# An RWKV-and-FFN kernel on one core: another order for its ramp, and GpSimd's constants in another order

## The chip, the cores and the metric

The kernel runs on one core of one Trainium2 chip. Its time is the device time of one execution in microseconds (us). Before the change the median of 3 runs is 554.37 us (554.30 to 554.86). The engines are named as the profile names them: PE (TensorE matmul; PEld is its weight load), DVE (VectorE), ACT (ScalarE), POOL (GpSimd), SP (SyncE). SP, POOL and ACT also issue transfers; "SPq" marks such an issue.

## The reference, cut to what matters

```python
for t in range(768):                       # B=4, H=8, D=48
    cur = einsum('bhd,bhe->bhde', u * kt, vt)
    y[:, :, t] = einsum('bhd,bhde->bhe', rt, state + cur)
    state = wt[..., None] * state + einsum('bhd,bhe->bhde', kt, vt)
x = y.transpose(0, 2, 1, 3).reshape(3072, 384)
h = x @ w_in                               # 384 x 2048
out = (h * sigmoid(1.702 * h)) @ w_out     # 2048 x 384
```

A linear recurrence with a decay per channel, and then a feed-forward layer over all 3072 tokens, all in float32.

## The kernel before, in words

The sequence is cut into 24 chunks of 128 tokens, 6 per batch entry. `chunk(t)` (L208) is a generator of 12 steps; the order calls one step with each token `a`t. Steps 1 and 2 scan the decays on DVE (L221 and L227, with the constants `d1r` and `d1f`) and form r·k (`rku`, L234); step 3 makes the scaled k and r (`kq`, L242 and L243); step 4 is PE's `ps_d` (L249: r·k times `hm`, the masks with u); step 5 copies that to `s` (L252) and decays the state (L259); step 6 transposes k (`ps_t`, L265) and ACT copies it to `kt` (L267); step 7 is ACT's `am`, eight diagonals (L274); step 8 is `ps_u`, k·v (L281 and L282), and the new state (L287); step 9 is `ps_s`, k·q (L293); step 10 puts `ps_s` into `am` above the diagonal (DVE, L296, twice); step 11 is `ps_y` (L306, and L313 where there is a state); step 12 splits `ps_y` into two float32r parts in `x` (ACT L191, DVE L192). `measure` (token `m`, L197) is bookkeeping of ranges on ACT.

The FFN is cut into tasks, each one slice f of 128 hidden units for 2, 3 or 4 chunks of tokens. `g`j is the first product of task j (PE, L343 to L345, nine matmuls), `h`j the GELU in two parts (ACT L354 and L355, DVE L356), `y`j the second product (PE, L369 to L371, nine matmuls). Two PSUM buffers hold first products, so `g`j+2 waits for both ACT reads of `h`j. The first tasks are 256 tokens wide. Before a group's tasks may run, small transfers fill 16-row strips of `x` from other rows of it (`fill_x`, L331, tokens `x1` for chunks 0 and 1, `x3` for chunks 2 and 3).

The weights come as packed 64-bit numbers in twelve pieces (even ones w_in, odd ones w_out). Token `f`i issues piece i's transfer into one of three staging buffers `st` (L161 or L163); tokens `w`i convert it in four steps: ACT L177 and L178, DVE L180 and L183, ACT L185 (`wih` or `woh`), DVE L187 (`wil` or `wol`). `l`t issues a chunk's loads (`wkr_t` on SP and POOL, or on SP and ACT for chunk 0; `v_t` on SP), `M` the two small transfers of the masks into `hm` (L424, L425), `u` that of `u_sb`.

All of this is laid out by hand: the string `RAMP` is a list of tokens, executed in that order until task 42, and `rest()` goes on by rule from there, leaving out what the string has done. Every engine executes its own instructions in the order in which the tokens emit them, so the string fixes the order on each engine and each issuing queue. The constants ahead of the string (`ident`, `after`, `hm`, `d1r`, `d1f`, `acc`) are written by POOL and are not part of it.

Of the kernel before, what the change touches and what calls it, by code (L numbers as in the profile page):

```python
# [8 lines left out]
F32 = mybir.dt.float32  # L9
F32R = mybir.dt.float32r  # L10
BF16 = mybir.dt.bfloat16
# [11 lines left out]
NP = H // 2  # L23
R = 2 * D
HB = 64
R2 = HB + D
C = P
CB = S // C
NT = NTOK // C
CW = C + 1  # L30
# [30 lines left out]

FIRST = 42
RAMP = """
l0 l0 M a0 l1 a0 a0 a0 a0 m0 a0 a1 a1 a1 l0 f0 m0 a0 a0 a0 a0 a1 a1 w0 m1 l2 w0 a2 a0 l1 a0 a1 a1 f1 a1 w0 a1
a2 l3 a2 w1 m1 f2 m2 m2 a2 a2 w0 a1 f3 w1 a3 a2 a1 a1 w2 a2 a3 w2 w1 l2 l3 x1 a2 w2 w1 a2 a3 a3 a3 g1 g0 a2 w2
m3 w3 a2 l4 h0 a4 a2 a3 w3 a3 a3 a4 g2 m3 w3 l4 a3 f4 a3 w3 h1 h2 w4 w4 a4 y0 a3 f5 f6 w5 g3 a3 w4 g4 y1 f7 w4
h3 w5 a4 a4 y2 h4 w6 g5 h5 a4 w5 y3 y4 x3 g7 w5 g6 w6 w7 h6 h7 w7 f8 y5 g8 w6 y7 a4 h8 y6 w6 a4 w7 g9 f9 g10
h9 w8 a4 y8 g11 w7 w8 h10 h11 y9 g12 w9 l5 g13 y10 y11 w8 w9 h12 f10 g14 f11 h13 y12 w8 h14 w9 y13 g16 w10 y14
w9 g15 h16 g18 a4 h15 m4 g17 w11 w10 h17 a5 m4 a4 y15 h18 a5 l6 l6 y16 y17 w10 g19 h19 l5 g20 a5 w11 a5 h20
w10 g21 u m5 a5 a5 a6 y18 y19 m5 w11 w11 h21 y20 g22 y21 a4 a6 a5 l7 a6 a5 a5 m6 a5 h22 a6 g23 h23 y22 a6 a5  # L70
a5 a7 a6 a6 l7 g24 a7 a6 a6 g25 x5 h24 a7 a7 m6 y23 a6 g26 l8 m7 a6 a7 a8 l8 a7 h25 h26 y24 a6 a7 a8 a8 g27
y25 g28 a7 a7 h28 h27 m7 y26 g30 a7 g29 y27 m8 h29 l9 g31 h30 y28 l9 y29 a8 a7 g32 l10 a8 h31 m8 a9 g33 a9 a8
y30 a9 h32 h33 y31 g34 a8 l10 y32 y33 m9 h34 g35 y34 h35 a7 g36 h36 g37 a8 a8 h37 g38 y35 a8 g39 a9 y36 a8 a9
y37 h38 a8 l11 m9 y38 h39 g40 x8 a9 g41 l11 h40 h41 y39
"""
WIDE = 512
assert sum(CHUNKS) == NT
# [3 lines left out]
def rwkv_ffn_kernel(ctx: ExitStack, tc, wkr, vp, vrk, ub, w_in, w_out, masks, vt, uc, out):  # L81
    nc = tc.nc
    V, A, G, T = nc.vector, nc.scalar, nc.gpsimd, nc.tensor

    cp = ctx.enter_context(tc.tile_pool(name="cp", bufs=1))
# [6 lines left out]
    at = fast.enter_context(tc.tile_pool(name="at", bufs=1))  # L92


    ident = cp.tile([P, P], F32, name="ident")
    make_identity(nc, ident)
    after = cp.tile([P, C], F32, name="after")
# [7 lines left out]
    G.memset(hm, 0.0)  # L105
    u_heads = hm[:, 2:].rearrange("r (p h) -> r p h", h=2)
    u_sb = cp.tile([P, DM], F32, name="u_sb")
    d1r = cp.tile([R2, NP, CW], BF16, name="d1r")
    G.memset(d1r, 0.0)
    G.memset(d1r[:, :, C : C + 1], 1.0)  # L110
    d1f = cp.tile([R2, NP, CW], F32, name="d1f")
    G.memset(d1f, 0.0)

    def by_head(dst, src, other=None):

# [465 lines left out]
```

## Time and profile before

| | |
|---|---|
| median of 3 runs | 554.37 us |
| the profiled execution | 553.65 us, its span 552.1 us |
| PE busy | 527.5 us (96%), 4038 matmuls |
| DVE, ACT busy | 288.6 us (52%), 291.0 us (53%) |
| PE first busy | 8.35 us |
| last wait of PE | ends at 66.19 us |
| last matmul of the FFN | starts at 545.54 us |
| transfers | 48.17 MB, DMA engines full in most of the first 65 us |

The span runs from the first to the last instruction of the execution. A mean share hides the stages here: in the first 66 us PE waits in many places while DVE and ACT work nearly without a pause from about 40 us on; after that PE is never idle until the last 7 us.

### The profile page before, as it was taken

The numbers are of one execution on the slowest core, as the hardware profiler recorded it, in microseconds if no ns is written. First come the engines' busy times: TensorE is split into PE (matmuls) and PEld (weight loads), VectorE is DVE, ScalarE is ACT, GpSimd is POOL, SyncE is SP. The second block draws the span as 40 slices with busy tenths as digits, with TensorE's granted clock in tenths as the row PEclk, the third lists the DMA queues.
The fourth block names the chain that finished last, engine by engine and source line by source line (L and its number), as shares of the span: only waits on it lengthen the run. The fifth ranks groups of instructions, "written<-read, shape, count | busy, mean of one in ns | idle before, by whom it ended". The sixth has DMA issues, their size and how long they took to land.

```text
span 552.1 us, 10054 instructions
## 1 busy us (share of the span) xinstructions
PE 527.5 (96%) x4038; PEld 493.7 (89%) x4038; DVE 288.6 (52%) x470; ACT 291.0 (53%) x686; POOL 34.6 (6%) x75
## 2 busy tenths in 40 slices
PE   1978999999999999999999999999999999999995
PEld 1857999988999999999999999999999999999995
DVE  4889977956643445536445445436445345321210
ACT  3778988656654364455454453455453563423222
POOL 3120210001001000000001000010001000010000
PEclk9999999999999999999999999999999999999998
DMA  8979797305632133143143241242242300011001
GB/s 176 248 186 214 174 230 183 67 1 130 180 94 59 37 93 60 36 115 99 39 93 81 78 94 34 61 114 72 67 94 55 104 1 1 2 23 43 1 0 49
DMA packets 18854, 48.17 MB, mean 87 GB/s; under 512 B 3312, under 2 KB 10064, under 8 KB 18800
## 3 DMA queue, kind: packets, MB, share of 16 engines
q1 hardware_dynamic: 15376, 36.02, 25.6%
q0 software_dynamic: 3296, 11.13, 10.0%
q8 instruction: 34, 0.56, 0.5%
q10 hardware_dynamic: 128, 0.30, 0.2%
q14 instruction: 20, 0.16, 0.1%
HBM read 40.36 MB, written 4.72 MB: 82 GB/s over the span
## 4 chain that ended last, share of the span: by engine, by line
PE 89%; DVE 4%; DMA 3%; issue 1%; ACT 1%; POOL 1%; SPq 0%; DVEq 0%; POOLq 0%
PE po L369 14%; PE ph L343 12%; PE ph L345 12%; PE ph L344 12%; PE po L371 12%; PE po L370 12%; PE ps_y L306 4%; PE ps_s L293 4%; PE ps_y L313 4%; DMA st<-in_w_out 3%; PE ps_u L281 1%; PE ps_t L265 1%; DVE st L180 1%; PE ps_d L249 1%; DVE c L183 1%
## 5 line engine op out<-in xcount | busy, mean ns | idle before, releaser
L356 DVE TENSOR_TENSOR gl<-gf,gh 128x384 fp32r<-128x384 f32 (+2 forms) x138 | 72.5, 529 | 209.0 <-ACT gf L355 208.5
L354 ACT ACTIVATE gh<-ph 128x384 fp32r<-128x384 f32 (+2 forms) x138 | 64.7, 469 | 195.6 <-PE ph L345 190.6
L369 PE MATMUL po<-gh,woh 128*128 128x384 f32 (+2 forms) x414 | 140.4, 339 | 0.0
L343 PE MATMUL ph<-x,wih 128*128 128x384 f32 (+2 forms) x414 | 135.5, 327 | 0.0
L345 PE MATMUL ph<-x,wil 128*128 128x384 f32 (+2 forms) x414 | 134.5, 325 | 0.0
L344 PE MATMUL ph<-x,wih 128*128 128x384 f32 (+2 forms) x414 | 134.4, 325 | 0.0
L371 PE MATMUL po<-gl,woh 128*128 128x384 f32 (+2 forms) x414 | 133.9, 324 | 0.3 <-DVE gl L356 0.3
L370 PE MATMUL po<-gh,wol 128*128 128x384 f32 (+2 forms) x414 | 134.1, 324 | 0.0
L369 PEld LDWEIGHTS po<-gh,woh 128*128 128x128 f32 x414 | 78.0, 188 | 6.6 <-issue 2.8
L343 PEld LDWEIGHTS ph<-x,wih 128*128 128x128 f32 x414 | 78.8, 190 | 1.7 <-issue 0.6
L345 PEld LDWEIGHTS ph<-x,wil 128*128 128x128 f32 x414 | 78.7, 190 | 0.8
L344 PEld LDWEIGHTS ph<-x,wih 128*128 128x128 f32 x414 | 78.7, 190 | 0.7
L371 PEld LDWEIGHTS po<-gl,woh 128*128 128x128 f32 x414 | 78.0, 188 | 1.3 <-DVE gl L356 0.5
L370 PEld LDWEIGHTS po<-gh,wol 128*128 128x128 f32 x414 | 78.2, 189 | 0.6
L355 ACT ACTIVATE gf<-ph 128x384 f32<-128x384 f32 (+2 forms) x138 | 64.0, 464 | 0.0
L274 ACT ACTIVATE am<-ident,s 128x128 f32<-128x128 f32 x192 | 58.9, 401 | 0.0
L221 DVE TENSOR_TENSOR_SCAN lp<-wkr_t,d1r 112x516 f32<-112x516 f32 x24 | 29.4, 1224 | 8.1 <-POOL d1r L110 4.8
L296 DVE COPY_PREDICATED am<-after,ps_s 128x512 f32<-128x512 int32 x48 | 32.4, 729 | 1.6 <-PE ps_s L293 1.6
L293 PE MATMUL ps_s<-kq 48*128 48x128 f32 x384 | 31.4, 304 | 0.1
L306 PE MATMUL ps_y<-am,v_t 128*64 128x128 f32 (+1 forms) x384 | 29.3, 291 | 2.3 <-DVE am L296 1.2
L293 PEld LDWEIGHTS ps_s<-kq 48*128 48x128 f32 x384 | 26.2, 204 | 5.2 <-issue 4.1
L306 PEld LDWEIGHTS ps_y<-am,v_t 128*64 128x64 f32 (+1 forms) x384 | 22.3, 136 | 8.2 <-DVE rk_t L237 2.2
(62 smaller groups left out, 483.3 us busy)
## 6 DMA issues: line engine op xcount, KB each, us to landing
wkr_t<-in_wkr SPq DMA_DIRECT2D x23, 385.2 KB, 5.8
wkr_t<-in_wkr POOLq DMA_DIRECT2D x23, 288.9 KB, 5.8
st<-in_w_out SPq DMA_DIRECT2D x6, 1024.0 KB, 11.8
rk_t<-in_vrk SPq DMA_DIRECT2D x16, 384.0 KB, 4.6
v_t<-in_vrk SPq DMA_DIRECT2D x24, 192.0 KB, 6.1
out_t<-ob SPq DMA_DIRECT2D x18, 192.0 KB, 1.9
st<-in_w_in POOLq DMA_DIRECT2D x6, 384.0 KB, 7.8
st<-in_w_in SPq DMA_DIRECT2D x6, 384.0 KB, 10.8
```

The costliest lines, as they stand in the source:

```text
L274: A.activation(x_[:, p], ident, AF.Copy, scale=s[:, 2 * p + h : 2 * p + h + 1])
L293: T.matmul(ps[h][:, p], kf[head(h), p], qf[head(h), p], start=True, stop=True)
L306: T.matmul(ps[at_ : at_ + m, p], v_[:, c : c + m], am[h][:, p], start=p == 0, stop=sf is None and p == NP - 1, skip_group_check=True,)
L343: T.matmul(ph, h_, xs[i][:, 0, c, cs], start=c == 0, stop=False)
L344: T.matmul(ph, h_, xs[i][:, 1, c, cs], start=False, stop=False)
L345: T.matmul(ph, l_, xs[i][:, 0, c, cs], start=False, stop=c == NM - 1)
L354: A.activation(gh, ph, AF.Gelu_apprx_sigmoid, scale=1.0 / W_SCALE)
L355: A.activation(gf, ph, AF.Gelu_apprx_sigmoid, scale=1.0 / W_SCALE)
L356: V.tensor_tensor(gl, gf, gh.bitcast(F32), op=ALU.subtract)
L369: T.matmul(o, woh[:, f, ms], gh, start=first, stop=False, skip_group_check=True)
L370: T.matmul(o, wol[:, f, ms], gh, start=False, stop=False, skip_group_check=True)
L371: T.matmul(o, woh[:, f, ms], gl, start=False, stop=f == NF - 1, skip_group_check=True)
```

## The change

Two things. First, `RAMP` is another permutation of the same 349 tokens (the same count of every token, so the same work, and `rest()` goes on alike). The table itself tells a reader little; its first line was

```diff
-l0 l0 M a0 l1 a0 a0 a0 a0 m0 a0 a1 a1 a1 l0 f0 m0 a0 a0 a0 a0 a1 a1 w0 m1 l2 w0 a2 a0 l1 a0 a1 a1 f1 a1 w0 a1
+l0 l0 a0 a0 l0 a0 M a0 a0 l1 m0 a1 f0 l1 l2 a0 a0 a0 a0 a0 a0 m0 f1 a1 a0 w0 a1 a1 a1 a1 l3 w0 m1 a1 a2 a1 l2
...
@@ -92,6 +92,11 @@
     at = fast.enter_context(tc.tile_pool(name="at", bufs=1))
 
 
+    d1r = cp.tile([R2, NP, CW], BF16, name="d1r")
+    G.memset(d1r, 0.0)
+    G.memset(d1r[:, :, C : C + 1], 1.0)
+    d1f = cp.tile([R2, NP, CW], F32, name="d1f")
+    G.memset(d1f, 0.0)
     ident = cp.tile([P, P], F32, name="ident")
     make_identity(nc, ident)
     after = cp.tile([P, C], F32, name="after")
@@ -105,11 +110,6 @@
     G.memset(hm, 0.0)
     u_heads = hm[:, 2:].rearrange("r (p h) -> r p h", h=2)
     u_sb = cp.tile([P, DM], F32, name="u_sb")
-    d1r = cp.tile([R2, NP, CW], BF16, name="d1r")
-    G.memset(d1r, 0.0)
-    G.memset(d1r[:, :, C : C + 1], 1.0)
-    d1f = cp.tile([R2, NP, CW], F32, name="d1f")
-    G.memset(d1f, 0.0)
```

Second, POOL writes `d1r` and `d1f` ahead of `ident`, `after` and `hm`. The first scan reads `d1r`; the strip of ones in it (a memset of its own) still comes behind POOL's first three transfer issues in both kernels, but the two selections that finish `ident` and `after` now come behind it.

What the new string does to the queues and engines, at three places. The first is the start of SP's queue. `wkr_t` and `v_t` are the loads of the first chunks, `hm` the masks, `st` the first piece of w_in. Before:

```order
L117 DMA wkr_t<-in_wkr 64x517
L117 DMA wkr_t<-in_wkr 64x1024
L424 DMA hm<-in_masks 48x10
L425 DMA hm<-in_masks 48x10
L117 DMA wkr_t<-in_wkr 64x1541
L142 DMA v_t<-in_vrk 128x384
L161 DMA st<-in_w_in 48x2x1024
```

and now:

```order
L117 DMA wkr_t<-in_wkr 64x517
L117 DMA wkr_t<-in_wkr 64x1024
L142 DMA v_t<-in_vrk 128x384
L424 DMA hm<-in_masks 48x10
L425 DMA hm<-in_masks 48x10
L117 DMA wkr_t<-in_wkr 64x1541
L161 DMA st<-in_w_in 48x2x1024
```

Chunk 0's `v_t` has moved ahead of the masks and of chunk 1's `wkr_t`.

The second is DVE in chunk 1, from the end of its first scan on. `ps_s0` and `ps_s1` are the two halves of chunk 0's `ps_s`. Before:

```order
L225 RECIPROCAL d1f_90<-lp_142 112x4
L227 SCALAR_TENSOR_TENSOR lp_142<-wkr_t_116,d1f_90 112x516
L234 TENSOR_TENSOR rku_147<-wkr_t_116 112x512
L242 TENSOR_TENSOR kq_149<-wkr_t_116,lp_142 112x512
L243 TENSOR_TENSOR kq_149<-wkr_t_116,lp_142 112x512
L296 COPY_PREDICATED am_160<-after_81,ps_s0_181 128x512
L296 COPY_PREDICATED am_165<-after_81,ps_s1_182 128x512
L252 COPY s_146<-ps_d_193 128x8
```

and now:

```order
L225 RECIPROCAL d1f_79<-lp_136 112x4
L296 COPY_PREDICATED am_156<-after_86,ps_s0_177 128x512
L296 COPY_PREDICATED am_161<-after_86,ps_s1_178 128x512
L227 SCALAR_TENSOR_TENSOR lp_136<-wkr_t_130,d1f_79 112x516
L234 TENSOR_TENSOR rku_204<-wkr_t_130 112x512
L192 TENSOR_TENSOR x_206<-ps_y_189,x_206 112x4x128
L242 TENSOR_TENSOR kq_212<-wkr_t_130,lp_136 112x512
L243 TENSOR_TENSOR kq_212<-wkr_t_130,lp_136 112x512
L252 COPY s_203<-ps_d_215 128x8
```

Chunk 0's masking and its part of `x` now stand among chunk 1's steps instead of behind them.

The third is SP's queue around the fills of chunks 2 and 3. Before, pieces 5, 6 and 7, then the fills, then piece 8:

```order
L163 DMA st<-in_w_out 128x2x1024
L161 DMA st<-in_w_in 48x2x1024
L161 DMA st<-in_w_in 16x2x1024
L163 DMA st<-in_w_out 128x2x1024
L331 DMA x<-x 16x2x256 x3
L161 DMA st<-in_w_in 48x2x1024
L161 DMA st<-in_w_in 16x2x1024
```

and now pieces 5 and 6, `u_sb`, the fills, then pieces 7 and 8:

```order
L163 DMA st<-in_w_out 128x2x1024
L161 DMA st<-in_w_in 48x2x1024
L161 DMA st<-in_w_in 16x2x1024
L422 DMA u_sb<-in_ub 128x384
L331 DMA x<-x 16x2x256 x3
L163 DMA st<-in_w_out 128x2x1024
L161 DMA st<-in_w_in 48x2x1024
```

The fills have moved ahead of piece 7, and `u_sb` ahead of both. On PE, the fourth chunk's `ps_d` stood ahead of the first FFN products (`g1`, `g0`) and now stands behind them and behind chunk 2's `ps_y`; and from there on the FFN tasks stand closer together (`y0 g2 g3 ps_u ps_s y1 g4 ps_y g5 y2 y3 y4` where before it was `ps_u g2 ps_s y0 ps_y g3 g4 y1 ps_d y2 g5 ps_t y3 y4`).

## Rows read from the trace of the kernel before

**Rows 1.** Busy time by stretch: us, busy of each engine (instructions), clock, DMA, GB/s
```profile
core 0: us, PE busy (x) PEld busy (x) DVE busy (x) ACT busy (x) POOL busy (x), PEclk, DMA share, GB/s
8.35:40.88 32.53, 24.58 (x180) 20.70 (x180) 26.32 (x38) 24.07 (x53) 5.23 (x10) 1.00 0.90 214
...
48.50:66.50 18.00, 15.89 (x158) 14.36 (x157) 17.66 (x26) 17.62 (x37) 3.31 (x7) 1.00 0.76 188
66.50:500.00 433.50, 433.50 (x3383) 405.92 (x3382) 226.92 (x379) 228.20 (x557) 22.08 (x43) 1.00 0.32 78
```
**Rows 2.** Timeline of PE: start, us, the instruction [idle before it]
```profile
40.88 1.87 PE L249 MATMUL ps_d<-hm,rku 112*128 112x2 f32 x8 [2.03 <-DVE sf L287]
42.62 0.56 PE L343 MATMUL ph<-x,wih 128*128 128x256 f32 x1
...
45.75 0.41 PE L345 MATMUL ph<-x,wil 128*128 128x256 f32 x1
...
46.15 0.28 PE L344 MATMUL ph<-x,wih 128*128 128x256 f32 x1
...
47.49 1.08 PE L313 MATMUL ps_y<-kq,sf 48*48 48x128 f32 x16
...
60.97 0.95 PE L249 MATMUL ps_d<-hm,rku 112*128 112x2 f32 x8
```
**Rows 3.** Timeline of all engines from 2 to 18 us
```profile
2.84 0.42 SPq L425 DMA_DIRECT2D hm<-in_masks  x1
...
4.75 1.23 DVE L221 TENSOR_TENSOR_SCAN lp<-wkr_t,d1r 112x516 f32<-112x516 f32 x1 [4.75 <-POOL d1r L110]
...
8.35 1.84 PE L249 MATMUL ps_d<-hm,rku 112*128 112x2 f32 x8 [8.35 <-DMA hm<-in_masks]
...
12.36 1.23 DVE L221 TENSOR_TENSOR_SCAN lp<-wkr_t,d1r 112x516 f32<-112x516 f32 x1 [1.96 <-DMA wkr_t<-in_wkr]
...
14.10 0.31 PE L281 MATMUL ps_u<-v_t,kt 128*64 128x48 f32 x1 [3.06 <-DMA v_t<-in_vrk]
...
17.27 1.34 DVE L296 COPY_PREDICATED am<-after,ps_s 128x512 f32<-128x512 int32 x2 [0.42 <-PE ps_s L293]
```
**Rows 4.** Transfers issued from 3.2 to 4.5 us: KB each, us to landing
```profile
v_t<-in_vrk SPq DMA_DIRECT2D x1, 192.0 KB, 9.8
hm<-in_masks SPq DMA_DIRECT2D x1, 1.9 KB, 5.4
```
**Rows 5.** Timeline of SP and ACT: the fills, and pieces 4 and 7
```profile
36.47 2.08 SPq L331 DMA_DIRECT2D x<-x  x3
...
54.97 1.16 ACT L177 ACTIVATE st<-st 128x1024 int32<-128x1024 uint32 x1
...
59.85 0.39 SPq L163 DMA_DIRECT2D st<-in_w_out  x1
...
66.45 1.16 ACT L177 ACTIVATE st<-st 128x1024 int32<-128x1024 uint32 x1
```
**Rows 6.** Transfers issued near 38, at 59.85 and 70.26, and near 41 us
```profile
x<-x SPq DMA_DIRECT2D x2, 32.0 KB, 2.0
...
st<-in_w_out SPq DMA_DIRECT2D x1, 1024.0 KB, 5.4
...
st<-in_w_out SPq DMA_DIRECT2D x1, 1024.0 KB, 9.8
...
st<-in_w_out SPq DMA_DIRECT2D x1, 1024.0 KB, 13.3
st<-in_w_in SPq DMA_DIRECT2D x1, 128.0 KB, 10.5
```
**Rows 7.** Waits of PE from 48.5 to 66.5 us: total, times, longest
```profile
PE ps_y L306 <- DVE am L296: 1.2, 2, 1.0
PE ps_u L281 <- ACT kt L267: 0.6, 1, 0.6
PE po L371 <- DVE gl L356: 0.3, 1, 0.3
```

More of the change, by code (lines that the diff above doesn't have):

```diff
@@ L63 @@
 RAMP = """
-l0 l0 M a0 l1 a0 a0 a0 a0 m0 a0 a1 a1 a1 l0 f0 m0 a0 a0 a0 a0 a1 a1 w0 m1 l2 w0 a2 a0 l1 a0 a1 a1 f1 a1 w0 a1
[L65 to L74, printed above, removed]
+l0 l0 a0 a0 l0 a0 M a0 a0 l1 m0 a1 f0 l1 l2 a0 a0 a0 a0 a0 a0 m0 f1 a1 a0 w0 a1 a1 a1 a1 l3 w0 m1 a1 a2 a1 l2
+f2 w0 w1 a1 a2 a2 a2 a1 m1 a2 a2 m2 w1 w0 f3 a3 a1 l3 a2 a1 a2 a3 m2 w2 x1 w1 a2 a3 g0 m3 a2 w1 w2 w3 f4 h0 g1
+m3 w2 w3 l4 a2 a3 w2 h1 a2 w4 a3 a3 y0 w4 g2 h2 a3 g3 a3 w4 l4 a3 y1 w3 a3 w4 f5 w3 h3 g4 a3 f6 h4 g5 u y2 a3
+a4 y3 w5 w5 h5 w6 x3 a4 y4 g7 g6 h7 h6 w5 w5 g8 g9 y6 f7 y5 y7 w6 w7 h8 f8 g10 f9 h9 w6 w6 h10 y8 w7 f10 w8
+g12 g11 h11 w7 y9 y10 w7 h12 g13 a4 g14 w8 h13 w9 y12 y11 g16 h14 y13 a4 w8 w9 a4 g15 w8 h16 a4 g18 h15 w10
+y14 w9 h18 w10 g17 m4 f11 h17 a4 l5 w10 y15 a4 a4 w9 g19 y16 g20 a5 h19 a5 y17 w11 h20 g21 w11 m4 y18 a5 g22
+w11 a4 l6 a5 h21 y19 w10 y20 h22 a5 a5 a4 a5 a5 l7 a5 g24 l5 w11 m5 g23 a6 a5 y21 a4 a6 m5 h23 a5 a6 m6 a6 a7
+a7 y22 a5 h24 y23 l7 l6 a6 a6 g25 y24 a7 h25 a6 x5 g26 h26 g27 a6 a6 y25 h27 g28 a7 g30 l8 h28 y26 a7 y27 y28
+m6 a6 m7 a8 a7 g29 h29 l9 g31 a6 h30 a6 a7 a7 y29 a7 l9 l8 a7 h31 y30 g32 a8 h32 m7 a8 y31 g33 h33 a8 l10 a8
+g34 m8 a7 h34 a7 a9 a8 a9 y32 g35 a9 g36 a8 y33 h35 a9 m8 y34 a8 a8 y35 g37 h36 a9 g38 a8 h37 a8 l10 h38 g39
+l11 m9 a8 x8 y36 y37 h39 y38 a9 m9 l11 g40 h40 g41 y39 h41
 """
```

## The prediction, made before the changed kernel had run

> **What bounds the kernel now.** I read the table of busy time by stretch first, then the timeline, then PE's waits. The table [rows 1] shows the stages. From 66.5 to 500 us PE is busy for all 433.5 us while DVE and ACT need about 228 us each: there only PE's own work counts, and the change leaves its amount alone. From 48.5 to 66.5 us PE is busy 15.9 of 18.0 us, DVE and ACT 17.7 and 17.6: here PE waits for them. From 8.35 to 40.88 us PE is busy 24.6 of 32.5 us and the DMA engines are 90% taken. So the time after 66.5 us is fixed, and what the change can move is the moment at which PE has done the work it had done then.
>
> A second thing is in the timeline of PE [rows 2]. An FFN matmul of 256 columns takes 0.41 us at 45.75 us and 0.28 us at 46.15; `ps_d` takes 1.87 us at 40.88 and 0.95 at 60.97. The clock column says 1.00 in every stretch, but by the durations PE runs at its lower level (1.2 GHz) until 46.0 us and at 2.4 GHz afterwards. The rise came 5.1 us after PE began, at 40.88, to work without a break. Work done before the rise costs double, so an FFN that begins earlier saves less than the time by which it begins earlier.
>
> **POOL's constants.** The first scan waits for `d1r` until 4.75 us [rows 3]. Two selections less ahead of it bring it forward by some 0.5 us (my estimate: two of the nine instructions that POOL has ahead of it). That is worth nothing by itself: PE's first `ps_d` starts at 8.35 us and is released by the masks `hm`, whose second transfer was issued at 2.84 us and took 5.4 us [rows 3, 4], until 8.24 us. The masks are the cover; were it gone, the half microsecond would count in full.
>
> **The masks behind `v_t`.** In SP's new queue the 192 KB of chunk 0's `v_t` go ahead of `hm`. What they take there is read from two neighbours of the old queue: chunk 1's `wkr_t` releases DVE's scan at 12.36 us, the `v_t` right behind it releases PE at 14.10 [rows 3], 1.7 us apart. The masks' issue starts 0.6 us later, part of which this hides. I take 10.3 us for their landing, 2.1 us later than before. The bounds: delayed by the issue alone, 3.4 + 5.4 = 8.8 us; as slow as `v_t` was [rows 4], 3.4 + 9.8 = 13.2 us. What pays for it is that `v_t` no longer comes at 14 us: PE's `ps_u` waited 3.06 us for it [rows 3]. Now `ps_u` follows the masks: 10.4 + 1.7 (`ps_d`, as from 8.35 to the next matmul's start) + 1.0 (`ps_t`) + 0.6 (`kt`) = 13.7 us instead of 14.1, 0.4 us gained. `ps_s` then ends 0.4 us earlier too, and DVE masks chunk 0 from about 17.0 to 18.3 us instead of 17.27 to 18.6 [rows 3].
>
> The Trainium skill (DMA: Bandwidth & Descriptors, "Queues, rings and completion order") says that each DMA engine takes the descriptors of one issuing queue in order, but that a later transfer may finish before an earlier one. With the first half, that the masks stand behind `v_t`, the 1.7 us agree; by the second they could come at 8.8 us, and the sum would be that of the second rival.
>
> **From there to the first FFN product.** In the new order DVE masks chunk 0 before chunk 1's second scan. So chunk 1 is later, not earlier: scan 18.3 to 19.5, `rku` to 20.1, `kq` to 22.4 with the split of chunk 0's `x` in between. What is gained is that this split is out of the way, and the chunks behind have fewer detours. Behind `kq` DVE has twenty instructions until chunk 1's `x` (`s`, `sf`, a conversion's pair L180 and L183, chunk 2's scan, reciprocal, `sf`, second scan, `rku`, two `kq`, two maskings, `s`, `sf`, a pair and its last step L187, chunk 3's scan and reciprocal). At the 0.69 us that 26 took on a full DVE (18.0 us [rows 1]) that is 13.8 us, so 36.2, and with the split 36.9 us. The fills took 3.5 us from there: issued over 2.08 us, the last of three landing 2.0 us after its start [rows 5, 6]. So `g0` can start at about 40.4. Waits between these steps that I can't see (ACT's cast of chunk 1's `x` is due at 36.2 too) cost up to 1.1 us; I take 40.8.
>
> Before, `ps_d` of chunk 3 ran at 40.88 and the FFN began at 42.62 [rows 2]. Now `g0` and `g1` run at once: 18 matmuls at 0.22 us (as the 16 from 42.62 to 46.15), 4.0 us, to 44.8, then `ps_y` of chunk 2. With the clock rising 5.1 us after the start, at 45.9, its first half ends at 46.4 and its second (1.0) at 47.4; `ps_d`, now at the upper clock, 0.8: 48.2. Before, the same work ended at 48.5 (47.49 and 1.0). Gain so far 0.3 us. The clock's bounds: at 2.4 GHz from `g0` on, another 2.5 us less; rising 2 us later, 1.0 us more.
>
> **From 48.5 to 66.5 us.** Before, PE lost four waits here: 1.2 us in two for DVE's masking, 0.6 us for `kt`, 0.3 us for the last GELU part, 2.1 us in all [rows 7]. In the new order the same PE work stands further behind DVE: the GELU remainder `gl` of the second task is DVE's 53rd instruction instead of its 64th, and the task's second product comes after four first products instead of five. Going along DVE from 36.9 us: `gl` of task 0 at 45.4, wanted at 48.6; of task 1 at 49.7, wanted at 53.6; the masking of chunk 3 from 53.7, wanted at 55.8. None is late; the thinnest cover is 1 to 2 us (that masking, which also needs `am` from ACT behind a conversion). So I take all 2.1 us as gone.
>
> **What is late next.** Piece 7's transfer now stands on SP behind the fills of `x3`. Before, it was issued at 59.85 us, landed 5.4 us later, and ACT's conversion began at 66.45 without a wait [rows 5, 6]: 1.2 us to spare. Now: chunk 3's `ps_y` ends at about 57.5, cast and split take until 58.9, the fills' issues 2.1 us, so it is issued at 61.0 and lands at 66.4, while ACT is ready for it at 65.3 (58.2, two pairs at 2.2, three GELUs at 0.55, a cast of 1.0). ACT waits 1.1 us. PE has `g8 g9 y6 y5 y7` to do until 69.5 and wants task 8's GELU, due at 66.4 + 2.2 + 0.55 = 69.2. So a transfer of 5.4 us costs nothing, and every microsecond above 5.75 one. Piece 8 follows close behind and shares the DMA engines; I put 0.4 us for it (bounds 0 and, at the 13.3 us of [rows 6], 7.5).
>
> **The sum.** 0.3 + 2.1 - 0.4 = 2.0 us less. Against the profiled execution (553.65 us, of which 552.1 are the span) that is 551.65; the runs' median stands 0.7 us above that execution, so 552.4 us for the median.
>
> **The rivals.**
> 1. *The cover of piece 4 is gone.* Its conversion moves from 54.97 [rows 5] to about 48.0 us, with the transfer issued at 39 to 40. Before, piece 4 took 10.5 us (the w_in row of [rows 6]); so it lands at 50, ACT waits 2 us in front of chunk 3's `kt` and `am`, and 1.2 to 1.6 us of the waits of [rows 7] come back. Time 553.8 us: no change. For it: ACT has no pause there [rows 1]. Against: the piece stood behind a chunk's loads, and now it is ahead of them.
> 2. *The masks are not delayed.* Everything to the first product moves 1.5 us forward, and the clock with it: 550.9 us. For it: 1.9 KB are little. Against: they took 5.4 us behind other loads as well [rows 4].
> 3. *Piece 7 lands as late as its neighbours.* It is behind the fills now; at the 9.8 us of piece 9 [rows 6] it lands at 70.8, ACT stands in front of it with task 8's GELU behind, and PE idles 4.05 us in front of `g10` and `y8`. 4.05 - 2.4 = 1.65 us slower, 556.0 us. It decides from a landing of 8.2 us on (gain gone), 9.3 us for slower. For it: the two neighbours in [rows 6] took 9.8 and 13.3 us. Against: the piece itself took 5.4, and the queue ahead of it now holds less. Masks at 13.2 us would give 555.3.
>
> **How the numbers follow.** Forecast 0.44 (its own range 551.4 to 553.2 us), rival 1 0.23, rival 2 0.16, rival 3 together with late masks 0.17. Forecast and rival 2 are faster by over 0.2% (1.1 us, about what a measurement of this kernel can tell from no change): 0.60. Within it: rival 1, 0.23. Slower: 0.17. The range 550.5 to 555.3 takes in rival 2, the late masks and a clock that rises 2 us late; it leaves out rival 3 from 9.2 us on and a clock that is up from the start.
>
> **What would show it right or wrong.** PE's first `ps_d` at about 10.4 us, and `ps_u` at 13.7 with its wait on `kt`, not on `v_t`; the first FFN product at 40.8 and the clock's rise near 46; from 48.2 to 70 us no wait of PE above 0.3 us; PE's last wait ahead of less work done than before. Wrong: a first FFN product after 42.5 us, an ACT wait of over 2 us for piece 4 or piece 7, or PE waits after 70 us.

## The result, and the profile after

The change made the kernel slower. Its median is 557.47 us (555.46 to 558.56, 9 runs) against 554.37 us (553.42 to 555.74, 9 runs) for the kernel before: a ratio of 1.0047, 95% interval 1.0034 to 1.0061. Forecast was 552.4 us, with 0.17 for slower. The profiled execution took 555.46 us, its span 553.8; it is the fastest of the nine. Timed again, beside the experiments, the changed kernel took 555.35 us against 554.27: 1.0020, interval 1.0005 to 1.0035.

Where the time went is read first in the sums of PE's waits. This is the profile after; the columns are the group, total us, times, and the longest:

```profile
PE ps_d L249 <- DMA hm<-in_masks: 13.1, 1, 13.1
PE ps_d L249 <- DVE rku L234: 1.9, 1, 1.9
PE ps_u L281 <- ACT kt L267: 1.8, 3, 0.7
PE ph L343 <- ACT gf L355: 1.5, 2, 0.7
...
PE ph L343 <- DMA x<-x: 0.8, 2, 0.6
```

The first line is the change's price. PE's first matmul waits for the masks until 13.05 us; before, it started at 8.35 [rows 3]. The wait for `v_t` (3.06 us before [rows 3]) is gone, as the new order meant; the longer wait for the masks has taken its place. The timeline of all engines after, at the places of [rows 3]:

```profile
2.22 0.59 SPq L142 DMA_DIRECT2D v_t<-in_vrk  x1
...
2.85 0.43 SPq L424 DMA_DIRECT2D hm<-in_masks  x1
2.93 1.09 POOL L161 DMA_DIRECT2D st<-in_w_in  x2
3.33 0.59 SPq L425 DMA_DIRECT2D hm<-in_masks  x1
...
4.21 1.34 DVE L221 TENSOR_TENSOR_SCAN lp<-wkr_t,d1r 112x516 f32<-112x516 f32 x1 [4.21 <-POOL d1r L97]
...
13.05 1.84 PE L249 MATMUL ps_d<-hm,rku 112*128 112x2 f32 x8 [13.05 <-DMA hm<-in_masks]
...
14.93 0.17 DVE L252 COPY s<-ps_d 128x8 f32<-128x8 f32 x1 [6.11 <-PE ps_d L249]
15.10 1.23 DVE L221 TENSOR_TENSOR_SCAN lp<-wkr_t,d1r 112x516 f32<-112x516 f32 x1
...
16.36 0.34 PE L281 MATMUL ps_u<-v_t,kt 128*64 128x48 f32 x1 [0.62 <-ACT kt L267]
...
19.59 1.33 DVE L296 COPY_PREDICATED am<-after,ps_s 128x512 f32<-128x512 int32 x2 [3.04 <-PE ps_s L293]
```

The first scan does start 0.54 us sooner (4.21 instead of 4.75), and nothing comes of it: DVE is ready for `s` at 8.8 us (14.93 - 6.11) and stands until `ps_d` ends. Chunk 1's scan, queued behind that `s`, starts at 15.10 instead of 12.36, and the masks are not the only reason: chunk 1's `wkr_t` now stands behind `v_t` as well and landed at 14.45 us. What carries the lateness on is chunk 0's masking (19.59 instead of 17.27 us), which in the new order stands ahead of chunk 1's second scan. The transfers issued from 2.2 to 3.9 us (KB each, median us to landing) answer to [rows 4]:

```profile
st<-in_w_in POOLq DMA_DIRECT2D x1, 384.0 KB, 8.9
wkr_t<-in_wkr POOLq DMA_DIRECT2D x1, 288.9 KB, 6.9
v_t<-in_vrk SPq DMA_DIRECT2D x1, 192.0 KB, 7.9
...
hm<-in_masks SPq DMA_DIRECT2D x2, 1.9 KB, 9.2
```

`v_t` lands at 10.1 us, the masks' second transfer at 12.93 (3.33 + 9.6; the row has the median of two). Behind this start the kernel made up ground. The stretches of [rows 1] again:

```profile
core 0: us, PE busy (x) PEld busy (x) DVE busy (x) ACT busy (x) POOL busy (x), PEclk, DMA share, GB/s
8.35:40.88 32.53, 23.20 (x173) 19.76 (x174) 22.12 (x34) 21.03 (x48) 2.72 (x6) 1.00 0.92 195
...
48.50:66.50 18.00, 17.55 (x180) 16.30 (x174) 15.70 (x22) 15.37 (x33) 2.60 (x5) 1.00 0.93 210
66.50:500.00 433.50, 431.67 (x3369) 404.13 (x3369) 230.01 (x387) 230.67 (x559) 22.84 (x44) 1.00 0.33 79
```

From 48.5 to 66.5 us PE is busy 17.55 us instead of 15.89; past 66.5 us it lost 1.8 us, where it had lost nothing. On the timeline of PE, for [rows 2]:

```profile
42.72 0.55 PE L343 MATMUL ph<-x,wih 128*128 128x256 f32 x1 [0.57 <-DMA x<-x]
...
46.27 0.41 PE L344 MATMUL ph<-x,wih 128*128 128x256 f32 x1
46.48 0.36 PE L345 MATMUL ph<-x,wil 128*128 128x256 f32 x1
...
47.79 1.08 PE L313 MATMUL ps_y<-kq,sf 48*48 48x128 f32 x16
48.79 1.05 PE L249 MATMUL ps_d<-hm,rku 112*128 112x2 f32 x8
```

The FFN begins at 42.72 us, no earlier than before (42.62), but now `ps_d` of chunk 3 stands behind it. The matmuls shorten at 46.5 us: PE is at 2.4 GHz from there, near 46.0 before. SP and ACT at the pieces, for [rows 5]:

```profile
48.06 0.39 SPq L163 DMA_DIRECT2D st<-in_w_out  x1
...
63.48 1.11 SPq L163 DMA_DIRECT2D st<-in_w_out  x1
```

```profile
51.23 1.16 ACT L177 ACTIVATE st<-st 128x1024 int32<-128x1024 uint32 x1 [0.76 <-DMA st<-in_w_in]
62.25 1.17 ACT L177 ACTIVATE st<-st 128x1024 int32<-128x1024 uint32 x1 [1.50 <-DMA st<-in_w_out]
...
69.38 1.17 ACT L177 ACTIVATE st<-st 128x1024 int32<-128x1024 uint32 x1
```

Those are pieces 4, 5 and 7. Piece 5, issued at 48.06 us, took 14.2 us to land and kept ACT waiting 1.50 us; piece 7 (69.38) kept nobody waiting.

The span in one sum: PE's busy time went from 527.5 to 526.5 us; its idle time went from 24.6 to 27.3, of which the first wait is 4.7 more (8.35 to 13.05) and all others together 2.0 less. 4.7 - 2.0 - 1.0 = 1.7 us, from 552.1 to 553.8.

### The profile page after: what moved, and what is told of

It reads as the page before. It is cut to its first block, busy times and chain, and to the rows that moved or that the text cites. A ratio compares the mean times of both kernels' runs of the same rounds, so it can differ in the third digit from the quotient of the medians.

```text
span 553.8 us, 10061 instructions
## 1 busy us (share of the span) xinstructions
PE 526.5 (95%) x4038; PEld 493.4 (89%) x4038; DVE 287.4 (52%) x470; ACT 291.6 (53%) x686; POOL 35.6 (6%) x75
## 4 chain that ended last, share of the span: by engine, by line
PE 73%; DMA 2%; DVE 1%; ACT 0%; issue 0%; SPq 0%; DVEq 0%
PE po L369 12%; PE po L370 10%; PE po L371 10%; PE ph L343 10%; PE ph L345 10%; PE ph L344 10%; PE ps_s L293 4%; PE ps_y L306 3%; PE ps_y L313 3%; PE ps_u L281 1%; DMA wkr_t<-in_wkr 1%; PE ps_t L265 1%; DMA x<-x 1%; PE ps_u L282 0%; DVE lp L221 0%
## 5 line engine op out<-in xcount | busy, mean ns | idle before, releaser
L227 DVE TENSOR_TENSOR_SCAN lp<-wkr_t,d1f 112x516 f32<-112x516 f32 x24 | 29.4, 1224 | 0.1
```

## Experiments

The main theory called "masks" or "share": the masks are late because `v_t(0)` stands ahead of them on SP's queue while other queues' bulk is in flight. Its rivals: the new table itself is at fault ("ramp"), the constants are ("POOL"), or PE's clock ("clock"). Each timed run stands beside the kernel before on the same chip. The main ones (first `ps_d` and time are of profiled executions; the median is of the runs timed in rounds; the kernel before beside them had medians from 553.67 to 554.79, and each ratio is to its own):

| kernel | masks / constants | first `ps_d` us | profiled us | median us | ratio, 95% interval |
|---|---|---|---|---|---|
| before | first / old | 8.35 | 553.65 | 554.37 | |
| POOL's constants alone | first / new | 9.08 | 553.77 | 554.30 | 0.9999, 0.9987 to 1.0010 |
| `v_t(0)` ahead, in before | behind / old | 12.49, 10.35 | 556.48, 554.30 | 555.44 | 1.0019, 1.0007 to 1.0032 |
| the change | behind / new | 13.05 | 555.46 | 557.47 | 1.0047, 1.0034 to 1.0061 |
| the change, again | behind / new | 11.97, 12.35, 12.33 | 554.92, 556.25, 553.72 | 555.35 | 1.0020, 1.0005 to 1.0035 |
| new table alone | behind / old | 9.94, 10.35 | 552.99, 553.75 | 552.18 | 0.9973, 0.9951 to 0.9995 |
| masks first, in the change | first / new | 9.23 | 552.16 | 552.34 | 0.9975, 0.9955 to 0.9995 |
| both cures | first / old | 8.65 | 549.85 | 551.80 | 0.9955, 0.9940 to 0.9971 |
| masks behind `wkr_t(1)` | further behind / new | 14.39 | 558.07 | 557.50 | 1.0059, 1.0036 to 1.0082 |

**One part at a time.** Masks first, in the changed kernel: the string begins

```
-l0 l0 a0 a0 l0 a0 M a0 a0 l1
+l0 l0 M a0 a0 l0 a0 a0 a0 l1
```

> The changed kernel with the token M (the masks' two transfers) put back ahead of chunk 0's v_t, at the place it had before; everything else as changed. Theory 'masks' (the 3 us are lost because hm lands at 12.9 us instead of 8.2 and holds PE's first ps_d to 13.05): ps_d starts at about 8.3 us, ps_u by 12 us, the first FFN product by 41.5, and the time falls by 2.5 to 4.5 us to 553.0 to 555.0. Theory 'ramp' (the loss comes behind 50 us, where first products wait for the GELU because pieces 5, 7 and 8 land late): the time stays at 556 to 557.5.

Measured: masks at 9.1 us, first `ps_d` 9.23, first FFN product 38.99, 552.34 us, faster than I gave even "masks". Chunk 0's masking starts at 16.10 instead of 19.59 us, behind chunk 1's `wkr_t`, and the rest follows. One token turned a slower kernel into a faster one.

`v_t(0)` ahead of the masks, in the kernel before:

```
-l0 l0 M a0 l1 a0 a0 a0 a0 m0 a0 a1 a1 a1 l0 f0
+l0 l0 l0 M a0 l1 a0 a0 a0 a0 m0 a0 a1 a1 a1 f0
```

> The kernel before with only chunk 0's v_t moved ahead of the masks on SP. Theory 'masks': hm lands near 12.5 to 13 us, PE's first ps_d starts then, ps_u moves from 14.1 to about 16, and the time rises by 1.5 to 3 us to 556.0 to 557.5. Theory 'ramp': no change, 554.4.

Measured: masks at 12.3 us, 555.44 us, slower by 0.19% (0.07 to 0.32): between my two windows, "masks" in its sign and less than its size. So the token's place costs in the old table too. The constants in the new order alone (the diff's other part), and the table alone (that part undone):

> The kernel before with only POOL's constants in the new order. Theories 'masks' and 'ramp': the first scan 0.5 us earlier, PE's first ps_d still held by hm near 8.3 us, time 554.4 within 0.5. A third theory, 'POOL' (POOL's bulk transfers, issued 0.6 us earlier, crowd the masks): hm lands later than 9 us and the time rises by over 1 us.

> The changed kernel with POOL's constants in the old order, so the new table alone. Theory 'masks': POOL's bulk comes 0.6 us later, hm may land up to 1 us earlier, time 556.5 to 557.5. Theory 'POOL': hm lands near 10 us, time 554.5 to 555.5. Theory 'ramp': 557.5.

Measured: the constants alone changed nothing (554.30, masks at 8.94 us). The table alone, masks still behind `v_t(0)`, was faster: masks at 9.8 us, 552.18 us, below all three windows. So neither part alone makes the loss; the two together do.

**Both cures**, masks first and constants in the old order:

> The new table with the masks issued ahead of v_t(0), and GpSimd's constants in the order of the kernel before: both cures of the late masks at once. Theory 'share' (the masks land late when v_t stands ahead of them on SP's queue and GpSimd's bulk is in flight early): masks land at 8.0 to 8.8 us, first ps_d at 8.2 to 9.0, first FFN product at 38 to 39, median 551 to 552. Theory 'chain' (below some point the masks no longer set the end, since the FFN's waits for gf and x take what the ramp gives): ps_d at 8.2 to 9.0 too, but the first FFN product not before 39 and the median at 552.2 to 552.6, as with either cure alone.

Measured: 551.80 us, the best complete kernel here, 0.45% below before (0.29 to 0.60). Its waits of PE:

```profile
PE ps_d L249 <- DVE kq L242: 8.6, 1, 8.6
PE ps_d L249 <- DVE rku L234: 1.9, 1, 1.9
...
PE ph L343 <- ACT gf L355: 0.7, 1, 0.7
```

The view puts the first wait down to DVE's `kq`, but `ps_d` does not read `kq`: it reads `rku`, done at 8.05 us, and the masks, which landed at 8.5 us (issued at 2.85, 5.7 us to landing). So `ps_d`, at 8.65 us, still follows the masks, only sooner. The first FFN product starts at 38.85 us: "share" holds. In both runs with the masks first, chunk 0's masking (16.00 and 16.10 us) stands behind chunk 1's `wkr_t` and not behind the masks, so masks any earlier would not have helped it. With the first `ps_d` within 0.3 us of the kernel before, what the new table is worth by itself is 2.65 us of the medians.

**What delays the masks.** The changed kernel with one more memset ahead of POOL's constants, so that its bulk is issued later:

```
+    dly = cp.tile([R2, NP, CW], BF16, name="dly")
+    G.memset(dly, 0.0)
     d1r = cp.tile([R2, NP, CW], BF16, name="d1r")
```

> The changed kernel with one more memset, of a tile that nothing reads, ahead of GpSimd's constants: the scans' constants still stand first, but GpSimd's bulk is issued some 0.5 us later, near 2.8 us, where the kernel before has it. Theory 'share': masks land near 9.8 us, first ps_d near 10, median 552 to 553, as with the constants in the old order. Theory 'order' (not the moment of the bulk but something else in the new order of the constants keeps the masks): masks at 12 to 13.5 us, median 556.5 to 558.

> A second profile of the run with GpSimd's bulk delayed, whose masks landed at 12.4 us where the run with the constants in the old order had 9.8 and 10.3. If the landing is a matter of the two queues' timing to a tenth of a microsecond, it lies anywhere between 9.8 and 12.5; if the new order of the constants itself sets it, near 12.4 again.

Measured: POOL's first bulk transfer at 2.75 us (2.28 in the change, 2.86 before), but the first `ps_d` at 12.40 and 12.28 us; median 554.67 (552.01 to 557.20, ratio 1.0005, 0.9985 to 1.0024). The masks are inside the window of "order", the median in neither.

This does not clear the bulk, though, because the run did not put all of it back. GpSimd's next issue, the first piece of w_in, came at 3.40 us (2.93 in the change, 3.50 with the constants in the old order). What goes with the landing, in all eighteen profiles whose first `ps_d` waits for the masks, is which issue was done first, that one or the issue of the second mask transfer: this transfer landed behind the piece's first and larger part if its issue was done later, and ahead of it if it was done sooner. First the table alone (first `ps_d` at 9.94), then the first profile of the kernel before with `v_t(0)` ahead (12.49), both with the old constants:

```profile
3.33 0.54 SPq L425 DMA_DIRECT2D hm<-in_masks  x1
3.50 1.08 POOL L161 DMA_DIRECT2D st<-in_w_in  x2
```

```profile
3.32 0.93 SPq L425 DMA_DIRECT2D hm<-in_masks  x1
3.51 1.09 POOL L161 DMA_DIRECT2D st<-in_w_in  x2
```

POOL's row holds two issues, the first of which takes 0.59 us. In the first of these profiles SP was done 0.2 us before POOL (3.87 and 4.09 us), and the masks landed at 9.8 us, 1.8 us ahead of the piece. In the second SP was done 0.15 us after POOL, and the masks landed at 12.35 us, 0.2 us behind the piece. Ten profiles have the masks directly behind `v_t(0)`. In seven of them SP was done 0.15 to 0.4 us after POOL: the change's four, the two with the extra memset (SP's issue took 0.85 and 0.92 us there), and that one with the old constants. Their masks landed 0.2 to 1.0 us behind the piece. In the other three SP was done 0.2 to 0.3 us before POOL, and the masks landed 1.5 to 1.9 us ahead of it. So the new order of the constants works through the moment of GpSimd's issues, as far as these profiles go. I found this afterwards, and no run moved that one issue alone. Why SP's issue takes 0.49 us in one profile and 0.93 in another isn't shown.

The masks' transfers on ScalarE's queue instead:

```
-                nc.sync.dma_start(hm[0:D], masks[0:D])
-                nc.sync.dma_start(hm[HB:R2], masks[D:R])
+                nc.scalar.dma_start(hm[0:D], masks[0:D])
+                nc.scalar.dma_start(hm[HB:R2], masks[D:R])
```

> The changed kernel with the two mask transfers issued by ScalarE's queue (behind its two of wkr_t(0)), and nothing else changed: v_t(0) still stands third on SP's queue, GpSimd's bulk is issued at 2.3 us. Theory 'queue' (the masks are late because they share SP's queue with v_t(0)): masks land at 6 to 8.5 us, first ps_d at 8.2 to 9.2, median 551.5 to 552.7. Theory 'engines' (any small transfer is late once that much bulk is in flight, wherever it is queued): masks at 10 to 13 us, median 554.5 to 557.5.

Measured: 553.26 us (0.9968, 0.9950 to 0.9986). In its timeline:

```profile
2.29 0.33 ACTq L424 DMA_DIRECT2D hm<-in_masks  x1
2.65 0.44 ACTq L425 DMA_DIRECT2D hm<-in_masks  x1
...
10.21 1.84 PE L249 MATMUL ps_d<-hm,rku 112*128 112x2 f32 x8 [10.21 <-DMA hm<-in_masks]
```

Off SP's queue the masks come 1.8 to 2.8 us sooner than in the changed kernel, yet the second transfer still took 7.4 us for 1.9 KB, and landed 0.4 us behind GpSimd's `wkr_t`, issued ahead of it. The median lies between the two windows. Both theories have a part: SP's queue, and the traffic on the engines that all queues share.

A second profile of the kernel before with `v_t(0)` ahead, and of the table alone:

> A second profile of the kernel before with v_t(0) ahead of the masks, whose masks landed at 12.3 us although GpSimd's bulk is issued at 2.86 us as in the run of the table alone (9.8 and 10.3). If the landing is a matter of chance between the queues, it lies anywhere between 9.8 and 12.5; if something of this program sets it, near 12.3 again.

> A second profile of the new table with GpSimd's constants in the old order, whose runs spread from 550.5 to 556.9 us; its first profile had the masks at 9.8 us and 553.0 us. 'share': masks between 9 and 13 us, and the time 0.8 to 0.9 us longer for each us that they are later than 9.8. 'clock': masks near 9.8 and a time that differs by the clock.

Measured: first `ps_d` at 10.35 us in both, where the first profiles had 12.49 and 9.94. The landing behind `v_t(0)` differs between runs of one program by up to 2 us, with the order of the two issues as above. Two more profiles of the changed kernel, and it timed again:

> The changed kernel unchanged, one more profile: its first profile was the fastest of its 9 runs, 2 us below their median. Theory 'share': masks land at 12.5 to 15 us here too, and each us later costs 0.8 to 0.9 us of the time. Theory 'clock' (the 2 us between its runs are the clock's, not the masks'): masks at 12.9 again and a later or interrupted full clock.

> A third profile of the changed kernel, for the spread: 'share' expects masks at 12.5 to 15 us and a time that follows them, 'clock' the same masks and a time that follows the moment of the full clock.

> The changed kernel unchanged, timed in rounds beside the run with later masks. Theory 'chain': median 555 to 556.5, what its three profiles (masks at 12.0, 12.4 and 13.1 us, 554.9 to 556.3 us) give. Theory 'other' (something that those profiles don't show adds 1 to 2 us in most runs): 557 to 558 again.

Measured: first `ps_d` at 11.97, 12.35 and 12.33 us, times 554.92, 556.25 and 553.72, the median of the timed runs 555.35. The masks are a little earlier than the windows that I gave for them, the median is inside that of "chain", and "other" falls. In all four profiles the changed kernel has the masks late; the 2 us between its two medians (557.47 and 555.35) stay unexplained.

**No wait, and a longer one.** I meant to move the masks one place later on SP's queue:

```
-l0 l0 a0 a0 l0 a0 M a0 a0 l1
+l0 l0 a0 a0 l0 a0 a0 a0 l1 M
```

> The changed kernel with the masks one place later on SP's queue, behind v_t(0) and the second wkr_t piece too (385 KB more ahead of them). From nine profiles with the new table, 549.85 us at a first ps_d of 8.65 us to 555.46 at 13.05, the time grows by 1.2 us for each us of the first ps_d. Theory 'chain' (the first ps_d carries the whole ramp): masks at 14.5 to 16 us, and the profiled time at 540.7 + 1.21 x the start of the first ps_d, 558 to 560. Theory 'clock' (the profiles' differences are the full clock's moment, the masks only go along): masks at 14.5 to 16 too, the time at 555 to 557 as in the changed kernel.

The token came to stand behind the first `ps_d` in the program: the first chunk's masks were left out, and its `ps_d` read the cleared tile. So this run shows the time without any wait for the masks. Its timeline:

```profile
7.76 1.83 PE L249 MATMUL ps_d<-hm,rku 112*128 112x2 f32 x8 [7.76 <-DVE rku L234]
9.63 0.17 DVE L252 COPY s<-ps_d 128x8 f32<-128x8 f32 x1 [0.82 <-PE ps_d L249]
9.69 0.35 SPq L424 DMA_DIRECT2D hm<-in_masks  x1
```

Measured: 550.76 us (0.9946, 0.9926 to 0.9966), 4.6 us below the changed kernel on the same chip; the first `ps_d` starts 4.6 us earlier than in that kernel's profile there (7.76 and 12.33). In the medians the wait for the masks passes to the end one for one, and it is the whole loss. The two profiled executions agree in sign only (552.38 and 553.72): with SP's queue held up, ACT waited 5.4 us for pieces from 40 to 75 us, against 2.3 us in the changed kernel's first profile. Then the run that I had meant, with `wkr_t(1)` and `v_t(0)` both ahead of the masks:

```
-l0 l0 a0 a0 l0 a0 M a0 a0 l1 m0
+l0 l0 a0 a0 l0 l1 a0 M a0 a0 m0
```

> The dose that the run before missed (there the masks came behind the first ps_d in the program, so that ps_d read the cleared tile and waited for no masks at all: the first chunk's masks were left out). Here the masks are still ahead of the first ps_d in the program, but behind v_t(0) and the 385 KB of wkr_t(1) on SP's queue. Theory 'chain' (the time follows the first ps_d one for one): masks at 13.5 to 16 us, the time 1 to 3.5 us above the changed kernel's, 556.5 to 559 us. Theory 'slowest' (they land when the transfers in flight thin out, near 12.5 us, whatever stands ahead of them): masks at 12 to 13 us, 555 to 556.5.

Measured: first `ps_d` at 14.39 us, 557.50 us (554.42 to 558.74, 6 runs). "Chain" holds, "slowest" falls. Over the twelve profiles with the new table whose ramp is otherwise unchanged and whose first `ps_d` comes behind the masks, a line through time and first `ps_d` is 541.2 us + 1.15 per us, and no profile lies further than 1.7 us from it. It rests on the whole stretch from 8.65 to 14.39 us: the changed kernel's own four, from 11.97 to 13.05 us, scatter too much (553.72 to 556.25) to show a slope by themselves. It gives 550.8 us at the 8.35 us of before, which took 553.65.

**Two tries at more.** In the kernel before, `v_t(0)` directly behind the masks (`l0 l0 M l0 a0 l1`):

> The kernel before with v_t(0) directly behind the masks and ahead of the second wkr_t piece. Theory 'share': masks land at 7.5 to 8.8 us as before, v_t some 1 to 2 us sooner than the 14.1 us of before, ps_u at 12 to 13 instead of 13.7, and the median at 553.2 to 554.3, since the first chunk's ps_d sets most of the chain. Theory 'v_t' (the new table's gain is v_t's place, not the rest of the table): median 552 to 552.6.

Measured: `ps_u` at 11.90 us instead of 14.10, but chunk 1's `ps_d` then waits 3.1 us for `rku`, whose `wkr_t` is one place later: 554.92 us, 1.0014 (1.0003 to 1.0026), above the window of either theory. `v_t`'s place is not the table's gain.

With both cures, chunk 4's loads behind piece 5 (`f5 l4 l4 w3` in place of two earlier `l4`):

> As the run with both cures, and the two fills of wkr_t(4) and v_t(4) moved behind the sixth FFN piece on SP's queue. Theory 'piece' (the waits for gf and of ScalarE for pieces 4 to 6 come from bulk queued ahead of them): ScalarE's wait for piece 5 falls from 1.5 us to under 0.5, the waits ph <- gf go, and the median lies 0.5 to 1.0 us below the run with both cures. Theory 'buffer' (piece 5 waits for the st buffer, not for the queue): no difference beyond 0.3 us.

Measured: 553.74 us, 0.9989 (0.9972 to 1.0006), worse than both cures. ACT's waits from 40 to 75 us, this run and then both cures:

```profile
ACT st L177 <- DMA st<-in_w_in: 4.8, 2, 3.3
ACT st L177 <- DMA st<-in_w_out: 1.7, 1, 1.7
```

```profile
ACT st L177 <- DMA st<-in_w_in: 1.1, 2, 0.9
ACT st L177 <- DMA st<-in_w_out: 1.0, 1, 1.0
```

The pieces came later, not sooner: "piece" falls, and why isn't settled.

## Why the prediction was wrong, step by step

- **The bound.** Right in that the end follows the moment at which PE gets through the ramp. Not quite right in that the time after 66.5 us is fixed: 1.8 us of waits moved there.
- **POOL's constants.** Alone worth nothing, as said, and measured so (0.9999). But the step counted only the half microsecond of the first scan, and in the cover that it named, the masks, it failed: it took them as given, while the same edit brings GpSimd's bulk ahead of them (issued at 2.28 and 2.93 us instead of 2.86 and 3.51). The masks are late where it does: the first `ps_d` is some 0.7 us later where they are first on the queue (8.35 and 8.65 us against 9.08 and 9.23), some 2 us later behind `v_t(0)` in the new table (9.94 and 10.35 against 11.97 to 13.05). The one late profile with the old constants (12.49) is the one in which SP's issue was done after POOL's too.
- **The masks behind `v_t`.** This is the step that failed and turned the sign: the term for the masks' landing. I took 10.3 us; it was 12.93, close to the upper bound of 13.2. The 1.7 us came from the gap between two landings on a queue that was already delivering, and I took the gap for what 192 KB cost. The row beside it had 9.8 us from issue to landing, and `v_t(0)` itself now took 7.9. And the sum counted only what stands ahead on SP's queue, while in the late profiles the masks land with GpSimd's bulk. The prediction's own figure for masks at 13.2 us, 555.3, is one for the median; it is close to the second median (555.35) and 2.2 us below the first (557.47), so that agreement is in part luck. That late masks would cost about as much as they are late was right; their size and their chance (a share of 0.17) were wrong.
- **The page's rule.** No masks queued behind `v_t(0)` came as early as those ahead of it, and in the changed kernel they landed 2.8 us after it (12.93 and 10.1 us). I had read only that a later transfer may finish before an earlier one. The same section (the Trainium skill, DMA: Bandwidth & Descriptors, "Queues, rings and completion order") goes on that a transfer's completion mark lands only after every earlier write of that DMA engine, across its queues. By that rule the masks wait for other queues' bulk as well, and two things agree with it: the run with the masks on ScalarE's queue, where 1.9 KB took 7.4 us with no `v_t` ahead, and the ten profiles in which the masks land behind whichever bulk of GpSimd was issued before them. No run here shows the marks themselves.
- **From `ps_d` on.** Right: `ps_u` 3.31 us behind the start of `ps_d` (3.3 forecast), the masking of chunk 0 6.5 us behind it (6.6), the first FFN product 29.7 (30.4). The clock rose 3.8 us behind the first FFN product (5.1 taken from one trace; the last section shows that it was no fixed delay).
- **The 2.1 us of waits.** The three waits of [rows 7] shrank or went, as forecast, but others came: `ph` for `gf` 1.5 us, `kt` still 0.5; the 0.8 us for `x` are mostly (0.57) the fills at 42.72 us, ahead of this stretch. Half of the wait for `gf` (0.74) comes at 67.88 us, behind ACT's wait of 1.50 us for piece 5 at 62.25, which no rival named, and half (0.75) only at 146.15 us; it was piece 4 (0.76 us here) and piece 7 (nothing) that I priced.
- **The sum.** Forecast were 2.05 us later at the first `ps_d` and 4.05 less behind it. Measured in the profile: 4.7 later, 3.0 less. So 2.65 of the 3.7 us of error are the masks, 1.05 lie behind the first `ps_d`, where the waits for `gf` came in place of others. On top, the first median stood 2.0 us above the profiled execution, where I took 0.7 from the kernel before; that part of the miss isn't explained.
- **The rivals.** The second, masks not delayed, 550.9 us, comes nearest to the run with both cures (551.80): the new table is worth what was forecast for it, if the masks are kept out of its way.

## What to carry to other kernels

A small transfer that the first instruction of the chain waits for belongs at the head of its queue; put 192 KB ahead of it, and look for its price in what such a transfer takes from issue to landing in the trace, and in the bulk that other queues issue before it, not in the gap between two landings (directly behind `v_t(0)`, the masks here landed 0.9 to 3.5 us after it). When a reordering wins in its middle and loses at its start, one run without the suspected wait tells the two apart. Two edits of which neither alone does harm can share a victim: run each alone and both together.

## What the runs showed of the hardware

The same 1.9 KB took from 4.2 us (before) to 10.5 us (masks behind `wkr_t(1)`) from issue to landing, and 4.3 and 7.4 us on a queue with no `v_t` ahead. Behind one and the same `v_t`, an issue done 0.2 us ahead of another queue's bulk or 0.2 us after it went with landings some 2 us apart (9.8 to 10.2 us and 11.8 to 12.9).

SP's queue stood still from 3.3 to 9.7 us in the run without the masks' wait, with the weights' first piece and chunk 1's `v_t` behind it, and that run was the fastest of all in the median.

PE's clock differed between profiles of one program. In the changed kernel's first profile the scores `ps_s` of chunk 2 ran at the lower level, in its fourth at the upper one (0.42 and 0.27 us each); first that of the first profile, then that of the fourth:

```profile
39.17 2.98 PE L293 MATMUL ps_s<-kq 48*128 48x128 f32 x16
```

```profile
38.16 0.48 PE L293 MATMUL ps_s<-kq 48*128 48x128 f32 x2
39.36 1.16 PE L293 MATMUL ps_s<-kq 48*128 48x128 f32 x14 [0.71 <-DVE x L192]
41.73 0.55 PE L343 MATMUL ph<-x,wih 128*128 128x256 f32 x1 [1.21 <-DMA x<-x]
```

In the fourth PE had worked without a break since chunk 2's `ps_d` at 30.97 us, and the clock rose within `ps_u` at 37.7 us. It was still up behind the pause of 0.71 us and fell within the one of 1.21 us. In the first PE had worked from 31.68 to 42.15 us with no pause over 0.12 us, longer than in the fourth, and the clock rose only at 46.5. By its windows (the stretch, its length, PE's busy time and matmuls, the clock, the DMA share, GB/s):

```profile
38.00:40.00 2.00, 1.28 (x20) 1.00 0.74 286
40.00:42.00 2.00, 0.79 (x9) 0.79 0.33 87
42.00:44.00 2.00, 2.00 (x10) 0.50 0.95 191
```

PE's busy time is 524.9 us there and 526.5 in the first profile, with the same matmuls. So up to 1.6 us of PE's work in one kernel goes with the clock, about as much as the change itself cost. The time doesn't simply follow it (the third profile has 525.0 us busy and took 556.25 us, the longest of the four), but a single profile of a ramp can mislead.
